# Seven products of half blocks in place of eight for the later batches' softmax times w_in

## The chip, the cores and the metric

The kernel runs on one NeuronCore of a Trainium2 chip. The metric is device microseconds (us) of one execution. The kernel before takes 716.05 us, the median of four runs that lie between 715.83 and 716.17 us.

## The reference

Two layers follow each other. The first is attention across channels: per batch `b` (4 batches, N = 6080 rows, C = 256 channels), the columns of q and k are normalised over the rows, `s = kn.T @ qn / tau` is a 256 x 256 matrix, a softmax over its last axis gives `a`, and the result is `v @ a`. The second layer works on all 24,320 rows:

```python
qn = q / (norm(q, axis=1) + 1e-6);  kn = k / (norm(k, axis=1) + 1e-6)
a  = softmax(kn.transpose(0, 2, 1) @ qn / tau, axis=-1)      # 4 x 256 x 256
x  = (v @ a).reshape(24320, 256)
h  = x @ w_in                                                # 256 -> 2048
g  = s * relu(h)**2 + b
out = g @ w_out                                              # 2048 -> 256
```

## The kernel before, in words

**Folding.** `v @ a @ w_in` is computed as `v @ (a @ w_in)`. For each batch the kernel makes one folded weight `wa`, 256 x 2048 in fp16, held as 128 partitions x 2 row halves x 2048 columns, and then never forms `x`. A batch's `e` (the exponentials, fp16, held transposed in the tile `eT`) is multiplied with `w_in`, and the row sums' reciprocals `rs` scale the result when it is read out of PSUM (the accumulator memory [...] that VectorE and ScalarE read).

**The main loop.** The rows are cut into 48 groups of 512 (the last has 256). A group is 16 steps; step `s` is group `s // 16`, place `m = s % 16`. A step does, in this order on TensorE:

- `mm1` (line 667): two matmuls of 512 columns that give one 128-row slice of `h` from `wa` and the transposed `v`;
- seven of the 112 matmuls of 128 columns (line 838) with which the group before is multiplied by `w_out`. That product already uses a seven-product scheme (`seven_items`): seven products X, Z, X, Y, X, Z, X of 16 matmuls each, with four sums S1 to S4 of blocks of `g` and four combinations T1, T2, T3, N4 of blocks of `w_out`. It starts at m = 3 and ends at m = 2 of the next group;
- what the table `side` holds for this step: the attention work of the next batch.

ScalarE does one relu of 1024 columns out of PSUM at each odd m (line 677), and at m = 3 and m = 5 a square besides (line 688). VectorE does three squares of 2048 columns per group (m = 0, 8, 12; line 690), the four sums S1 to S4 (m = 2, 3, 6, 10; lines 765 to 771), and the seven read-outs of the `w_out` products (line 695: at m = 5, 7, 9, 12, 14 and at m = 0 and 2 of the next group, by the count of 16 matmuls per product and seven per step). `h` has two PSUM tiles, so `mm1` of an even m needs the relu of four steps before; relu writes to two buffers `r16`, each freed by a square.

**The order of work.** Each engine runs its instructions in the order in which the program writes them (`po`, `keep_in_program_order`), one queue per engine; there is no planner. `at_step(s, f)` puts a piece of work at the end of step `s`. For batches 1 to 3 the Gram matrix `k.T @ q`, the norms and then `finish_ops` are laid out this way. With `first_group[b]` = 11, 23, 35 and `w1 = 16 * first_group[b] - 3`, the finish begins at `w1 - 54`, and its i-th piece stands at `w1 - 54 + 1 + FIN[i]`, or 3 steps apart after the end of `FIN`.

**The finish of a later batch.** The pieces are: copy the Gram matrix out, sum the norms, four activations for the inverse norms, scale, two exponentials, `sums` (row sums and their reciprocal, at `FIN` 22, which is m = 14), and then eight folds (`fold_one`): four blocks of 512 columns of `w_in` times two row halves. Each fold is two matmuls of 128 x 128 by 128 x 512 (line 328), accumulated over the two halves of the contraction in one PSUM bank, and one read-out that multiplies by `rs` and writes fp16 into `wa`: by ScalarE for m = 0 (line 321), by VectorE for m = 1 (line 323). The bank comes from the pool `ps_gram`, which has a single buffer, so a fold can start only when the read-out before it is done. The folds stand at m = 1, 4, 7, 10, 13, 0, 3 and 6 (`FIN[-1] + 3 * ...`). The result is first needed by `mm1` of group `first_group[b]`.

**Buffers.** The last three chunks of batch 0's norms (`NLATE` = 3) square q and k into `late_pool`, three buffers of 4096 bytes per partition that nothing uses afterwards.

Of the kernel before, what the change touches and what calls it, by code (L numbers as in the profile page):

```python
# [17 lines left out]
def kernel(  # L18
# [37 lines left out]
    def po(ins):  # L56

        tc.keep_in_program_order(ins)
        return ins

    def pool(name, bufs, **kw):
        return ctx.enter_context(tc.tile_pool(name=name, bufs=bufs, **kw))
# [3 lines left out]
    wpool = pool("wpool", 1)  # L66
    qk_pool = pool("qk_pool", 8)
    sq_pool = pool("sq_pool", 2)
    late_pool = pool("late_pool", NLATE)
    f3_pool = pool("f3_pool", 13)  # L70
    sm_pool = pool("sm", 1)
    apool = pool("apool", 2)
# [3 lines left out]
    gpool = pool("gpool", 2)  # L76
    spool = pool("spool", 1)
    upool = pool("upool", 4)
    opool = pool("opool", 2)

    ps_gram = pool("ps_gram", 1, space=PSUM)
# [29 lines left out]
    class Gram:  # L111
# [45 lines left out]
        def norm_ops(self, c):  # L157

            qc, kc = self.tiles[c]
            _, np_, jc = self.chunks[c]  # L160
            st = {}

            at_end = self.b == 0 and c >= len(self.chunks) - NLATE

            def squares(a, js):
                def f():
                    if "sq" not in st:
                        st["sq"] = (late_pool if at_end else sq_pool).tile(
                            [P, 2, JC, C], FP16, tag="sq", name="sq")
                    if a == 1 and at_end and c == len(self.chunks) - 1:  # L170
                        po(nc.vector.tensor_mul(
                            st["sq"][:np_, 1, js, :], kc[:np_, js, :], kc[:np_, js, :]))
                    elif a == 0 and (self.b > 0 or at_end or c % 2 == 0):
                        po(nc.vector.tensor_mul(  # L174
                            st["sq"][:np_, 0, js, :], qc[:np_, js, :], qc[:np_, js, :]))
                    else:
                        po(nc.scalar.activation(  # L177
                            out=st["sq"][:np_, a, js, :], in_=(qc, kc)[a][:np_, js, :],
                            func=AF.Square))
                return f  # L180

            def fold(half, arrays, last):
                def f():
                    src = st["f", 2 * half] if 2 * half < jc else st["sq"]
                    if ("f", half) not in st:
                        if last:
                            t = f3_pool.tile([P, 2, 1, C], FP16, tag="f3", name="f3")
                        else:
                            t = sq_pool.tile([P, 2, half, C], FP16, tag=f"f{half}", name="f")
                        st["f", half] = t  # L190
                    po(nc.vector.tensor_add(  # L191
                        st["f", half][:np_, arrays], src[:np_, arrays, :half, :],
                        src[:np_, arrays, half : 2 * half, :]))
                    if last and c == 0:
                        self.first = st["f", half]
                    if last and (c == 0 or self.b > 0 and c == len(self.chunks) - 1):
                        for rows in self.rows:
                            rows.append((st["f", half], np_, 1))
                return f

            def into_first():

                dst, src = self.first[:np_], st["f", 1][:np_]
                if self.b == 0:
                    po(nc.vector.tensor_add(dst, dst, src))  # L205
                else:
                    po(nc.gpsimd.dma_start(out=dst, in_=src, accum_op=ALU.add))  # L207

            def unfolded(a):
                self.rows[a].append((st["sq"], np_, jc))  # L210

            ops = []
            for h in range(0, jc, 4):
                js = slice(h, min(h + 4, jc))
                ops += [squares(1, js), squares(0, js)]
            if at_end:
                def rows(a):
                    if a == 0 or jc == 2:
                        return unfolded(a)
                    half = sq_pool.tile([P, 2, 2, C], FP16, tag="f2", name="half")  # L220
                    po(nc.vector.tensor_add(half[:np_, 1], st["sq"][:np_, 1, :2], st["sq"][:np_, 1, 2:]))
                    self.rows[1].append((half, np_, 2))
                return ops + [rows]
            if jc == 8:
                ops += [fold(4, slice(0, 1), False), fold(4, slice(1, 2), False)]
            ops += [fold(2, slice(0, 2), False), fold(1, slice(0, 2), True)]
            return ops + [into_first] if 0 < c < len(self.chunks) - 1 else ops
# [24 lines left out]
        def finish_ops(self):  # L252
# [3 lines left out]
            def inverse(a=None):  # L256

                n = C + CH if a is None else (CH, C)[a]

                def part(i):  # L260
                    if i == 0:
                        st["r", a] = sm_pool.tile([P, n], FP32, tag=f"r{a}", name=f"r{a}")
                        if a is None:
                            st["r", 1], st["r", 0] = st["r", a][:, :C], st["r", a][:, C:]
                    r = st["r", a]
                    func, kw = [(AF.Ln, dict(bias=tiny)), (AF.Exp, dict(scale=0.5)),
                                (AF.Ln, dict(bias=eps)), (AF.Exp, dict(scale=-1.0))][i]
                    sums = self.n_all if a is None else self.n_ps[a]
                    po(nc.scalar.activation(out=r, in_=r if i else sums, func=func, **kw))  # L269
                    if i == 3 and a != 1 and inv_tau != 1.0:  # L270
                        po(nc.vector.tensor_scalar_mul(
                            out=st["r", 0], in0=st["r", 0], scalar1=inv_tau))

                return [lambda i=i: part(i) for i in range(4)]
# [78 lines left out]
            def fold_one(f0, n, m):  # L353
                def f():
                    wa_ps = self.bank("wa_ps", CH, C).rearrange("p a c -> p (a c)")[:, :n]
                    fold_mm(f0, n, m, wa_ps)
                    if self.b == 0 and f0 == 2 * NW and m == 1:
                        return at_step(5, lambda: scaled(f0, n, m, wa_ps))
                    scaled(f0, n, m, wa_ps)
                return f  # L360

            if self.b == 0:
                blocks = [(2 * P, 2 * P), (4 * P, 2 * P), (6 * P, 2 * P), (2 * NW, NW), (3 * NW, NW)]
            else:
                blocks = [(f0, NW) for f0 in range(0, Dff, NW)]
            folds = [fold_one(f0, n, m) for f0, n in blocks for m in range(CH)]
            if self.b == 0:
                return [norms(1), *inverse(1), norms(0), *inverse(0), lambda: scale(CH),
                        lambda: first_block(2 * P)] + folds
            return [copy_out, norms_both, *inverse(), scale, lambda: exps(0), lambda: exps(1),  # L370
                    sums] + folds

        def bank(self, name, a, b):

# [189 lines left out]
        po(nc.scalar.copy(out=T[:, ts(i, 2), :], in_=w[:, 0, :, :P] if T is T2 else w[:, 0, :, P:]))  # L564


    side, early = {}, {}

    def at_step(s, f):
        side.setdefault(int(s), []).append(f)  # L570


    FIN = (0, 3, 5, 7, 9, 11, 13, 17, 19, 22)
    first_group = [b * N // TG for b in range(B)]
    FOLDS = (0, 0, 1, 1, 3, 3, 5, 5, 8, 8)
    for i, f in enumerate(folds):
# [30 lines left out]
    for b in range(1, B):  # L607
        gr = grams[b]
        w0 = first_group[b - 1] * FT + (26 if b == 1 else 6)
        w1 = first_group[b] * FT - 3  # L610
        NCH = len(gr.chunks)
        fin_len = 54
        span = (w1 - fin_len) - w0 - 12
        n = NCH * JC
        for c in range(NCH):
            sc = w0 + span * c * JC / n
            at_step(max(3, sc - 16), lambda gr=gr, c=c: gr.load(c))
            if c == 0:
                at_step(sc, gr.start)
            for j in range(JC):  # L620
                at_step(w0 + span * (c * JC + j) / n, lambda gr=gr, c=c, j=j: gr.mm(c, j))

            def norm_step(gr=gr, c=c, sc=sc):
                ops = gr.norm_ops(c)
                later = LATER.get((gr.b, c), {})
                for i, f in enumerate(ops):
                    at_step(int(sc) + 3 + i * 3 + later.get(i, 0), f)
            at_step(sc - 3, norm_step)

        def fin_step(gr=gr, s=w1 - fin_len):  # L630
            ops = gr.finish_ops()
            for i, f in enumerate(ops):
                at_step(int(s) + 1 + (FIN[i] if i < len(FIN) else FIN[-1] + 3 * (i - len(FIN) + 1)), f)
        at_step(w1 - fin_len - 12, fin_step)


# [298 lines left out]
```

## Time and profile before

| | |
|---|---|
| median of the runs shown | 716.05 us (715.83 to 716.17) |
| profiled execution | 716.16 us, its span 714.4 us |
| TensorE (PE) busy | 694.4 us, 97% of the span |
| weight loads (PEld) busy | 503.1 us, 70% |
| VectorE (DVE) busy | 623.2 us, 87% |
| ScalarE (ACT) busy | 545.7 us, 76% |
| granted TensorE clock | 0.997 of full speed |

The span runs from the first to the last instruction of the profiled execution; 1.8 us of that execution's time lie around it. "Busy" counts the time in which an engine works on an instruction. Consecutive instructions on an engine overlap a little (a VectorE row of 1.22 us is followed after 1.14 us), so a row's duration is somewhat more than the room it takes in its queue. Below, "starts" are given in us from the start of the span.

### The profile page before, as it was taken

What the parts mean: (1) busy time and instruction counts of PE and PEld (TensorE: products, weight loads), DVE (VectorE), ACT (ScalarE), POOL (GpSimd) and SP (SyncE); (2) the same over time, 40 slices, a digit from 0 to 9 for tenths busy, and PEclk for the clock granted to TensorE, in tenths of its full rate; (3) what the DMA queues carried; (4) which work ended last, traced back from release to release, by engine and by line L of the source; (5) the groups of instructions that cost most, each with busy time, mean ns of one, the idle gap of its engine ahead of it and who ended that gap; (6) DMA issues with size and microseconds to landing.
All of it is one profiled execution on the core that took longest, in us unless ns stands there. A gap on an engine that the chain in (4) does not pass through costs nothing.

```text
span 714.4 us, 17525 instructions
## 1 busy us (share of the span) xinstructions
PE 694.4 (97%) x7437; PEld 503.1 (70%) x7437; DVE 623.2 (87%) x877; ACT 545.7 (76%) x593; POOL 111.0 (16%) x189
## 2 busy tenths in 40 slices
PE   4699999999999999999999999999999999999998
PEld 2456777776777777777677777777668777777777
DVE  4889999988888989998889899998887888888886
ACT  5789877787777777778777777777877777777875
POOL 4533132102102222101010222110000000000000
PEclk9999999999999999999999999999999999999999
DMA  9999998637575989445772888943323333321202
GB/s 234 207 259 172 172 175 133 132 77 126 103 132 109 132 139 148 105 89 102 138 142 50 148 134 147 132 90 82 94 63 75 94 71 75 97 61 46 82 31 75
DMA packets 87454, 83.47 MB, mean 117 GB/s; under 512 B 56304, under 2 KB 62384, under 8 KB 87376
## 3 DMA queue, kind: packets, MB, share of 16 engines
q0 software_dynamic: 26608, 43.40, 38.0%
q1 hardware_dynamic: 60192, 37.71, 21.8%
q8 instruction: 58, 0.95, 0.6%
q10 hardware_dynamic: 576, 1.25, 0.5%
q14 instruction: 20, 0.16, 0.1%
HBM read 78.91 MB, written 24.90 MB: 145 GB/s over the span
## 4 chain that ended last, share of the span: by engine, by line
PE 95%; DMA 3%; ACT 1%; DVE 1%; issue 0%; DVEq 0%; ACTq 0%
PE h_ps L667 46%; PE o_ps L838 40%; PE s_ps L148 4%; PE wa_ps L328 2%; DMA qk<-in_k_dram 1%; DMA raw<-in_q_dram 1%; PE o_ps L742 1%; ACT sq L177 1%; PE o_ps L714 0%; DVE f L191 0%; ACT r L269 0%; PE n_ps L244 0%; ACT qk L139 0%; DVE f L205 0%; DVE sq L174 0%
## 5 line engine op out<-in xcount | busy, mean ns | idle before, releaser
L677 ACT ACTIVATE r<-h_ps 128x1024 f16<-128x1024 f32 (+1 forms) x384 | 388.8, 1014 | 148.8 <-PE h_ps L667 142.8
L667 PE MATMUL h_ps<-vT,wa 128*128 128x512 f16 (+7 forms) x1632 | 452.1, 364 | 0.5 <-ACT wa L321 0.5
L838 PEld LDWEIGHTS <-S 128*128 128x128 f16 x2944 | 198.0, 98 | 84.3
L838 PEld LDWEIGHTS <-g 128*128 128x128 f16 x2208 | 155.1, 98 | 74.2
L690 DVE TENSOR_TENSOR g<-r 128x2048 f16<-128x2048 f16 (+2 forms) x150 | 174.5, 1163 | 12.3 <-ACT r L677 11.9
L838 PE MATMUL o_ps<-T,S 128*128 128x128 f16 x2208 | 183.0, 219 | 0.0
L667 PEld LDWEIGHTS <-wa 128*128 128x128 f16 x1632 | 135.8, 98 | 19.7 <-ACT wa L321 1.0
L838 PE MATMUL o_ps<-w_out,g 128*128 128x128 f16 x1472 | 134.2, 219 | 0.0
L695 DVE SCALAR_TENSOR_TENSOR o_sb<-o_ps,s_out,u 128x256 f32<-128x256 f32 x138 | 66.3, 480 | 51.5 <-PE o_ps L838 49.5
L688 ACT ACTIVATE g<-r 128x1024 f16<-128x1024 f16 (+1 forms) x97 | 100.3, 1034 | 0.2
L148 PE MATMUL s_ps<-qk 128*128 128x256 f16 (+1 forms) x384 | 70.9, 286 | 14.9 <-ACT qk L139 9.3
L389 POOL DMA_DIRECT2D v<-in_v_dram x48 | 30.5, 637 | 264.4 <-DMA vT<-v 195.6
L695 DVE SCALAR_TENSOR_TENSOR u<-o_ps,s_out,rowconst 128x256 f32<-128x256 f32 x138 | 65.7, 476 | 0.0
L838 PE MATMUL o_ps<-w_out,S 128*128 128x128 f16 x736 | 63.5, 219 | 0.0
L838 PE MATMUL o_ps<-N,g 128*128 128x128 f16 x736 | 63.4, 219 | 0.0
L207 POOL DMA_DIRECT2D f<-f x30 | 26.4, 878 | 224.8 <-DVE f L191 175.2
L767 DVE TENSOR_TENSOR S<-S,g 128x2048 f16<-128x2048 f16 (+1 forms) x47 | 56.4, 1200 | 1.3
L177 ACT ACTIVATE sq<-qk 128x1024 f16<-128x1024 f16 (+2 forms) x53 | 54.5, 1041 | 3.9 <-DMA qk<-in_k_dram 2.4
L765 DVE TENSOR_TENSOR S<-g 128x2048 f16<-128x2048 f16 (+1 forms) x47 | 56.0, 1192 | 0.0
L771 DVE TENSOR_TENSOR S<-g,S 128x2048 f16<-128x2048 f16 x46 | 55.8, 1214 | 0.0
L769 DVE TENSOR_TENSOR S<-g 128x2048 f16<-128x2048 f16 x46 | 55.8, 1214 | 0.0
L148 PEld LDWEIGHTS <-qk 128*128 128x128 f16 (+1 forms) x384 | 32.5, 102 | 20.9 <-ACT qk L139 9.8
(83 smaller groups left out, 313.6 us busy)
## 6 DMA issues: line engine op xcount, KB each, us to landing
out_dram<-o_sb SPq DMA_DIRECT2D x43, 512.0 KB, 3.0
v<-in_v_dram POOLq DMA_DIRECT2D x47, 256.0 KB, 4.6
qk<-in_k_dram POOLq DMA_DIRECT2D x42, 256.0 KB, 6.8
qk<-in_q_dram POOLq DMA_DIRECT2D x42, 256.0 KB, 7.4
f<-f POOLq DMA_DIRECT2D x30, 128.0 KB, 3.1
vT<-v SPq DMA_TRANSPOSE x182, 2.9
w<-in_moe_w_out_dram POOLq DMA_DIRECT2D x4, 512.0 KB, 9.8
out_dram<-o_sb SPq DMA_DIRECT2D x8, 256.0 KB, 5.5
```

Source lines behind the costliest of these rows:

```text
L148: po(nc.tensor.matmul(self.s_ps[:, ch, :], qc[:np_, j, ts(ch, P)], kc[:np_, j, :], start=(c == 0 and j == 0 and ch == 0), stop=(c == len(s ...
L177: po(nc.scalar.activation(out=st["sq"][:np_, a, js, :], in_=(qc, kc)[a][:np_, js, :], func=AF.Square))
L667: po(nc.tensor.matmul(dst, wa[:, ci, ts(m, P)], src, start=(ci == 0), stop=(ci == CH - 1), skip_group_check=True))
L677: po(nc.scalar.activation(out=r16[:, :, i % 2, :n], in_=h_tiles.pop((g, i))[:, :, :n], func=AF.Relu))
L688: po(nc.scalar.activation(out=dst, in_=src, func=AF.Square))
L690: po(nc.vector.tensor_mul(dst, src, src))
L695: po(nc.vector.scalar_tensor_tensor(out=dst, in0=src, scalar=s_out, op0=ALU.mult, in1=add, op1=ALU.add))
L765: po(nc.vector.tensor_add(T[1], A21, A22))
L767: po(nc.vector.tensor_sub(T[2], T[1], A11))
L769: po(nc.vector.tensor_sub(T[3], A11, A21))
L771: po(nc.vector.tensor_sub(T[4], A12, T[2]))
L838: po(nc.tensor.matmul(st[name][:, j, :], a()[:, i, ts(j, P)], w[:, i, :], start=first, stop=last, skip_group_check=True))
```

## The change

Only batches 1 to 3 change; batch 0 keeps its folds.

- A 256 x 256 matrix times a 256 x 1024 pair of column blocks is a product of 2 x 2 blocks: two row halves and two contraction halves of `e`, and the contraction halves and the lower and upper 1024 columns of `w_in`. It is now computed by seven block products in place of eight, in two parts `p` of 512 columns (`seven_folds(0)`, `seven_folds(1)`).
- Each product is one matmul of 512 columns and stands at its own step. A product that is not marked new accumulates onto what the bank holds, after that has been read out: products 1 to 4 add up in one bank, product 5 has a bank of its own (the pool still has one buffer), products 6 and 7 add up in one.
- Each product has one read-out. Products 1, 2 and 3 are kept as fp32 tiles `u1`, `u2`, `u3` (1 and 3 by ScalarE, 2 by VectorE); product 4 goes to `wa` by ScalarE; products 5, 6 and 7 go to `wa` by VectorE, which multiplies by `rs` and adds `u1`, `u3` or `u2` in one instruction.
- `half_sums` makes four sums of 128 x 128 blocks of `e` on VectorE, right after the reciprocal, per batch. `w_in_sums` makes four combinations of 128 x 1024 blocks of `w_in` on VectorE, once, during batch 1's finish, at steps 6, 8 (two of them) and 22 after the finish begins. They are stored in the buffers of `late_pool`, which now have one tag per late chunk and that chunk's own size.
- `FIN` gets 14 entries (25 to 55) for the 14 products: m = 1, 3, 7, 9, 11, 13, 15, the same in two consecutive groups. The last stands one step before group `first_group[b]` begins.

```diff
@@ -66,7 +66,7 @@
     wpool = pool("wpool", 1)
     qk_pool = pool("qk_pool", 8)
     sq_pool = pool("sq_pool", 2)
-    late_pool = pool("late_pool", NLATE)
+    late_pool = pool("late_pool", 1)
     f3_pool = pool("f3_pool", 13)
     sm_pool = pool("sm", 1)
     apool = pool("apool", 2)
@@ -76,6 +76,7 @@
     gpool = pool("gpool", 2)
     spool = pool("spool", 1)
     upool = pool("upool", 4)
+    fold_pool = pool("fold_pool", 1)
     opool = pool("opool", 2)
 
     ps_gram = pool("ps_gram", 1, space=PSUM)
@@ -165,8 +166,10 @@
             def squares(a, js):
                 def f():
                     if "sq" not in st:
-                        st["sq"] = (late_pool if at_end else sq_pool).tile(
-                            [P, 2, JC, C], FP16, tag="sq", name="sq")
+                        if at_end:
+                            st["sq"] = late_pool.tile([P, 2, jc, C], FP16, tag=f"sq{c}", name="sq")
+                        else:
+                            st["sq"] = sq_pool.tile([P, 2, JC, C], FP16, tag="sq", name="sq")
                     if a == 1 and at_end and c == len(self.chunks) - 1:
                         po(nc.vector.tensor_mul(
                             st["sq"][:np_, 1, js, :], kc[:np_, js, :], kc[:np_, js, :]))
@@ -359,16 +362,77 @@
                     scaled(f0, n, m, wa_ps)
                 return f
 
+            def half_sums():
+
+                A = lambda m, k: st["e"][:, k, ts(m, P)]
+                S = st["S"] = [fold_pool.tile([P, P], FP16, tag=f"S{n}", name=f"S{n}")
+                               for n in range(1, 5)]
+                po(nc.vector.tensor_add(S[0], A(1, 0), A(1, 1)))
+                po(nc.vector.tensor_sub(S[1], S[0], A(0, 0)))
+                po(nc.vector.tensor_sub(S[2], A(0, 0), A(1, 0)))
+                po(nc.vector.tensor_sub(S[3], A(0, 1), S[1]))
+
+            def seven_folds(p):
+
+                A = lambda m, k: st["e"][:, k, ts(m, P)]
+                B = lambda k, n: w_in16[:, k, ds(n * (Dff // 2) + p * NW, NW)]
+                T = lambda n: W[n][:, ts(p, NW)]
+                S = lambda n: st["S"][n - 1]
+                C_ = lambda m, n: self.wa[:, m, ds(n * (Dff // 2) + p * NW, NW)]
+                rs = lambda m: st["rs"][:, m : m + 1]
+                u = {}
+
+                def product(a, w, then, new=False):
+                    def f():
+                        if new:
+                            st["wa_ps"] = self.bank("wa_ps", CH, C).rearrange("p a c -> p (a c)")
+                        po(nc.tensor.matmul(st["wa_ps"], a(), w(), start=new, stop=True,
+                                            skip_group_check=True))
+                        then()
+                    return f
+
+                def keep(n, m):
+                    def f():
+                        u[n] = fold_pool.tile([P, NW], FP32, tag=f"u{n}", name=f"u{n}")
+                        if n == 2:
+                            po(nc.vector.tensor_scalar_mul(
+                                out=u[n], in0=st["wa_ps"], scalar1=rs(m)))
+                        else:
+                            po(nc.scalar.mul(out=u[n], in_=st["wa_ps"], mul=rs(m)))
+                    return f
+
+                def out(m, n, k=None):
+                    def f():
+                        if k is None:
+                            po(nc.scalar.mul(out=C_(m, n), in_=st["wa_ps"], mul=rs(m)))
+                        else:
+                            po(nc.vector.scalar_tensor_tensor(
+                                out=C_(m, n), in0=st["wa_ps"], scalar=rs(m), op0=ALU.mult,
+                                in1=u[k], op1=ALU.add))
+                    return f
+
+                return [
+                    product(lambda: A(0, 0), lambda: B(0, 0), keep(1, 0), True),
+                    product(lambda: S(2), lambda: T("T2"), keep(2, 0)),
+                    product(lambda: S(3), lambda: T("T3"), keep(3, 1)),
+                    product(lambda: A(1, 1), lambda: T("N4"), out(1, 0)),
+                    product(lambda: A(0, 1), lambda: B(1, 0), out(0, 0, 1), True),
+                    product(lambda: S(1), lambda: T("T1"), out(1, 1, 3), True),
+                    product(lambda: S(4), lambda: B(1, 1), out(0, 1, 2)),
+                ]
+
             if self.b == 0:
                 blocks = [(2 * P, 2 * P), (4 * P, 2 * P), (6 * P, 2 * P), (2 * NW, NW), (3 * NW, NW)]
-            else:
-                blocks = [(f0, NW) for f0 in range(0, Dff, NW)]
-            folds = [fold_one(f0, n, m) for f0, n in blocks for m in range(CH)]
-            if self.b == 0:
+                folds = [fold_one(f0, n, m) for f0, n in blocks for m in range(CH)]
                 return [norms(1), *inverse(1), norms(0), *inverse(0), lambda: scale(CH),
                         lambda: first_block(2 * P)] + folds
+
+            def sums_and_halves():
+                sums()
+                half_sums()
+
             return [copy_out, norms_both, *inverse(), scale, lambda: exps(0), lambda: exps(1),
-                    sums] + folds
+                    sums_and_halves] + seven_folds(0) + seven_folds(1)
 
         def bank(self, name, a, b):
 
@@ -564,13 +628,31 @@
         po(nc.scalar.copy(out=T[:, ts(i, 2), :], in_=w[:, 0, :, :P] if T is T2 else w[:, 0, :, P:]))
 
 
+    W = {}
+
+    def w_in_sums(i):
+
+        F = Dff // 2
+        B = lambda k, n: w_in16[:, k, ds(n * F, F)]
+        if not W:
+            c0, c1, c2 = range(NCH0 - NLATE, NCH0)
+            W["T1"] = late_pool.tile([P, F], FP16, tag=f"sq{c1}", name="T1w")
+            W["T2"] = late_pool.tile([P, F], FP16, tag=f"sq{c2}", name="T2w")
+            both = late_pool.tile([P, 2, F], FP16, tag=f"sq{c0}", name="TNw")
+            W["T3"], W["N4"] = both[:, 0], both[:, 1]
+        po([lambda: nc.vector.tensor_sub(W["T1"], B(0, 1), B(0, 0)),
+            lambda: nc.vector.tensor_sub(W["T2"], B(1, 1), W["T1"]),
+            lambda: nc.vector.tensor_sub(W["T3"], B(1, 1), B(0, 1)),
+            lambda: nc.vector.tensor_sub(W["N4"], B(1, 0), W["T2"])][i]())
+
     side, early = {}, {}
 
     def at_step(s, f):
         side.setdefault(int(s), []).append(f)
 
 
-    FIN = (0, 3, 5, 7, 9, 11, 13, 17, 19, 22)
+    FIN = (0, 3, 5, 7, 9, 11, 13, 17, 19, 22,
+           25, 27, 31, 33, 35, 37, 39, 41, 43, 47, 49, 51, 53, 55)
     first_group = [b * N // TG for b in range(B)]
     FOLDS = (0, 0, 1, 1, 3, 3, 5, 5, 8, 8)
     for i, f in enumerate(folds):
@@ -630,7 +712,10 @@
         def fin_step(gr=gr, s=w1 - fin_len):
             ops = gr.finish_ops()
             for i, f in enumerate(ops):
-                at_step(int(s) + 1 + (FIN[i] if i < len(FIN) else FIN[-1] + 3 * (i - len(FIN) + 1)), f)
+                at_step(int(s) + 1 + FIN[i], f)
+            if gr.b == 1:
+                for i, later in ((2, 6), (0, 8), (1, 8), (3, 22)):
+                    at_step(int(s) + later, lambda i=i: w_in_sums(i))
         at_step(w1 - fin_len - 12, fin_step)
```

## The prediction

> **What bounds the kernel now.** I read the page first, then TensorE's waits, the groups by shape, the busy time of the fold stage, and the timelines around the first fold of batch 1.
>
> ```profile
> span 714.4 us, 17525 instructions
> ...
> PE 694.4 (97%) x7437; PEld 503.1 (70%) x7437; DVE 623.2 (87%) x877; ACT 545.7 (76%) x593; POOL 111.0 (16%) x189
> ...
> PE   4699999999999999999999999999999999999998
> ...
> PE 95%; DMA 3%; ACT 1%; DVE 1%; issue 0%; DVEq 0%; ACTq 0%
> ```
>
> TensorE is full from the third slice on, and the chain that ended last is 95% TensorE. The 20 us in which it is not busy lie in front: its waits, longest first in total, are five rows; these four and one of 0.3 us.
>
> ```profile
> PE s_ps L148 <- ACT qk L139: 9.3, 2, 7.5
> PE s_ps L148 <- DMA qk<-in_q_dram: 5.6, 6, 1.5
> PE n_ps L244 <- DVE half L221: 1.3, 1, 1.3
> PE h_ps L667 <- ACT wa L321: 0.5, 1, 0.5
> ```
>
> All belong to batch 0. The busy times in the stretch that holds batch 1's folds (us; PE, PEld, DVE, ACT, POOL) say the same, and show the room beside TensorE: about 5 us on VectorE, 8 on ScalarE.
>
> ```profile
> 163.40:193.90 30.50, 30.50 (x317) 20.83 (x315) 25.55 (x35) 22.17 (x25) 3.00 (x7) 1.00 0.65 121
> ```
>
> So a matmul removed here shortens the run by its own pace, as long as no read-out makes TensorE wait. Groups by shape (busy us, mean ns) give the durations:
>
> ```profile
> L690 DVE TENSOR_TENSOR g<-r 128x2048 f16<-128x2048 f16 x137 | 166.6, 1216 | 10.0 <-ACT r L677 9.7
> L695 DVE SCALAR_TENSOR_TENSOR o_sb<-o_ps,s_out,u 128x256 f32<-128x256 f32 x138 | 66.3, 480 | 51.5 <-PE o_ps L838 49.5
> L328 PE MATMUL wa_ps<-w_in,eT 128*128 128x512 f16 x56 | 16.3, 379 | 0.0
> L323 DVE TENSOR_SCALAR wa<-wa_ps,rs 128x512 f16<-128x512 f32 x14 | 10.4, 744 | 0.0
> L321 ACT ACTIVATE wa<-wa_ps,rs 128x512 f16<-128x512 f32 x14 | 9.6, 684 | 0.0
> L690 DVE TENSOR_TENSOR g<-r 128x1024 f16<-128x1024 f16 x9 | 6.2, 687 | 1.9 <-ACT r L677 1.8
> L695 DVE SCALAR_TENSOR_TENSOR o_sb<-o_ps,s_out,rowconst 128x512 f32<-128x512 f32 x2 | 1.4, 746 | 0.1
> ```
>
> The timeline of TensorE (start, length) shows a fold between two steps; the 379 ns of a matmul are latency, its pace is read from starts.
>
> ```profile
> 165.12 0.59 PE L667 MATMUL h_ps<-vT,wa 128*128 128x512 f16 x2
> 165.55 0.55 PE L838 MATMUL o_ps<-N,g 128*128 128x128 f16 x7
> 165.94 0.59 PE L328 MATMUL wa_ps<-w_in,eT 128*128 128x512 f16 x2
> 166.38 0.59 PE L667 MATMUL h_ps<-vT,wa 128*128 128x512 f16 x2
> ```
>
> From 165.94 to 166.38 (0.432 before rounding) are two matmuls: 0.216 each. A step without a fold is 0.432 for `mm1` plus 0.39 for seven small ones, 0.822.
>
> **What the skill says.** "TensorE: Matmul & The Clock Gate", section "Back-to-back issue gap", gives a 512-column matmul 512/2.4 + 2.5 = 216 ns; this trace agrees. "PSUM — Partial Sum Buffer", section "The four PSUM rules", allows a synchronised read of a partial sum inside an accumulation group, so products 2, 3, 4 and 7 may add onto a bank that has been read; each must wait for that read, and no run here shows it yet. "VectorE: DVE Perf Modes", section "Side-by-side: where the cycles go for N=2048 bf16", makes a 16-bit tensor_tensor two elements per cycle plus some 150 cycles: 1224 ns for 2048, the trace has 1216; for the 128-column half sums, which the trace lacks, I take (64 + 150)/0.96 = 223 ns as an estimate, between 0.15 (the reciprocal of 2 columns, 157 ns) and 0.42 (the 512-column row of line 690, 418 ns).
>
> **The change on TensorE.** Per batch 8 folds x 2 = 16 matmuls go, 2 parts x 7 = 14 come: two fewer. Three batches: 6 x 0.216 = **1.30 us less**. Each product keeps one weight load of 98 ns; loads lie beside matmuls (PEld 68% in that stretch) and six of them go too.
>
> **The read-outs.** Per batch ScalarE goes from four to six of 0.684 (0.57 of room, as the next row starts 0.1 before the end), VectorE from four to eight: two plain of 0.744, six with an added operand. Does the operand cost? At 256 columns rows of line 695 with `u` take 480 ns, with `rowconst` 476 to 482; so I price 512 columns at the 746 of the last row above (0.66 of room). VectorE's load per group in the fold stage, in room: three squares and four sums at 1.14 plus 0.12 for the dependent pair S1, S2, 8.1; seven read-outs at 0.395, 2.8; four fold read-outs at 0.66, 2.6: 13.5 us. A group lasts 16 x 0.822 + 7 x 0.216 = 14.66. It fits, with 1.1 to spare. ScalarE: eight relus at 0.92, two squares at 0.94, three read-outs at 0.57: 10.9.
>
> **Whether a product waits.** All products use the one bank, so each must find the read-out before it finished. Products are 0.216 + 2 x 0.822 = 1.86 us apart, except 3.50 between the second and third. I place them on the clock of batch 1, first product at 165.94 as before, each engine's queue in program order:
>
> - Product 1 (m = 1): ScalarE reads it after this step's relu, 166.67 to 167.35 as the fold there today. Product 2 starts at 167.80: 0.45 to spare.
> - Product 2 (m = 3): VectorE reads it behind S1 and S2, which follow the read-out of the last `w_out` product (167.18); 169.97 to 170.71. Product 3 at 171.31: 0.60.
> - Product 3 (m = 7): ScalarE is behind here, two squares at m = 3 and 5: relu at 171.33, read-out 172.25 to 172.94. Product 4 at 173.18: **0.24**, the least. Today's fold at m = 7 has it likewise:
>
> ```profile
> 171.78 1.01 ACT L677 ACTIVATE r<-h_ps 128x1024 f16<-128x1024 f32 x1
> 172.68 0.69 ACT L321 ACTIVATE wa<-wa_ps,rs 128x512 f16<-128x512 f32 x1
> ```
>
> - Product 4 (m = 9): read by 174.59, product 5 at 175.05: 0.46.
> - Product 5 (m = 11): behind S4, read 175.45 to 176.19, product 6 at 176.92: 0.73.
> - Product 6 (m = 13): behind the m = 12 read-out and square, read 177.64 to 178.38, product 7 at 178.79: 0.41.
> - Product 7 (m = 15): read by 179.91; the next part's product 1 at 180.65: 0.74.
>
> VectorE then waits again for the next group's last `w_out` product, so nothing is carried into part two or the next batch. Behind a late read-out would stand the m = 14 read-out and the squares, whose buffer the relu at m = 13 or m = 1 needs; they end more than 2 us before it. The last write into `wa` (about 1 us into the next group) concerns columns used at m = 12 to 15, 10 us later. The Gram bank is next needed seven steps on. No DMA or queue of SP or POOL moves. The stage makes no waits: 0.
>
> **The sums.** Half sums: 4 x 0.22 = 0.9 us per batch right after the reciprocal, where VectorE sits idle 1.24 us before 165.21. Hidden; without that cover they would put off S1 by 0.9. `w_in_sums`, once: four of 0.687 (0.60 of room). The last, at m = 13, falls before the same gap; the 0.3 that spill over end in the gap of 0.57 before 167.40. The other three (m = 13 and twice m = 15 of the group before, the second of the pair dependent, +0.12) come to 1.92 us from 150.22. The gaps there hold 1.25 (before 151.95) and 0.23 (before 153.71). S1 would begin at 154.46, not at
>
> ```profile
> 154.11 1.22 DVE L765 TENSOR_TENSOR S<-g 128x2048 f16<-128x2048 f16 x1
> 155.69 0.44 PE L838 MATMUL o_ps<-T,S 128*128 128x128 f16 x5
> ```
>
> so it ends at 155.68, while TensorE's first use of it stands at 155.69 with its weight load 0.05 ahead. I take a wait of **0.10 us**, once; bounds 0 and 0.4 (if the small gap gives nothing).
>
> **Sum.** Against its own execution (716.16; 714.4 of span and 1.8 around): -1.30 + 0.10 = -1.20, so 713.2 of span and 714.96; the median of the runs lies 0.11 lower, 716.05, so **714.85**, 0.17% less. `late_pool`'s three tags keep three buffers for three chunks: 0.
>
> **Rivals.**
> - *Handover waits eat part of the gain.* The 0.24 at product 4 and 0.41 at product 7 assume that a release costs nothing. For: a square waiting on a relu starts 0.03 after it, but TensorE waiting on ScalarE is seen only in batch 0. With 0.4 per release, product 4 waits 0.16 six times, about 0.9 in all: 715.8.
> - *VectorE becomes the bound, slower.* Place: the six three-operand read-outs per batch. If the fp32 `u` stream costs a pass of its own, three per group exceed the spare 1.1 us. Price: at 1.5 us each, 3 x 0.75 - 1.1 = 1.15 per group, six groups 6.9: 716.05 - 1.2 + 6.9, about 721.5. From 1.28 us each (1.6 over per group, 0.5 late, 3 us in all) the result is slower than before. Against: 480 against 476 ns at 256 columns.
> - *TensorE is not what sets the pace there*, and the saved matmuls turn into idle: 716.05. Against: 30.50 busy of 30.50.
>
> **How the numbers follow.** Forecast 0.65, own range 714.55 to 715.2; handover waits 0.20; no gain 0.03; VectorE bound 0.12. A measurement here tells about 0.2%, 1.43 us, from no change, and the whole matmul gain is 1.30: only the low tail of the forecast counts as faster, 0.14; slower is the VectorE case, 0.12; the rest, 0.74, is within 0.2%. The range, 714.4 to 716.5, holds all but the last case and a little of each edge.
>
> **What would show it.** Line 328's matmuls for batches 1 to 3 fall from 48 to 42 with 0.216 between starts; TensorE's waits gain no row above 0.2 us; three-operand read-outs near 0.75 us; VectorE's gap near 151 filled, a wait of about 0.1 us at 155.7. A TensorE wait on the kept tiles, on `wa` or at product 4, or read-outs above 1.1 us, would prove it wrong.

## The result, and the profile after

The changed kernel takes 715.09 us (median of 42 runs, 714.83 to 715.58) against 715.97 for the kernel before in the same sessions: 0.88 us less, ratio 0.9988 with a 95% interval of 0.9984 to 0.9993. That is within 0.2%, in the lower half of the forecast range (714.4 to 716.5) and inside the narrower one (714.55 to 715.2); the forecast was 714.85, a gain of 1.20.

The page of the changed kernel's profiled execution (715.08 us) begins:

```profile
span 713.3 us, 17540 instructions
...
PE 692.3 (97%) x7431; PEld 502.2 (70%) x7431; DVE 634.7 (89%) x905; ACT 548.5 (77%) x599; POOL 110.9 (16%) x189
```

TensorE has six matmuls less (7431 for 7437), VectorE 28 instructions and 11.5 us more, ScalarE six and 2.8 us more. The busy times of batch 1's fold stage, same columns as for the kernel before, show where the room went: VectorE from 25.55 to 28.50 us of 30.50.

```profile
163.40:193.90 30.50, 30.50 (x321) 21.05 (x319) 28.50 (x43) 23.80 (x28) 3.88 (x8) 1.00 0.62 124
```

Groups by shape of the changed kernel (busy us, mean ns): the read-outs that add an operand, the two kinds that are kept, the last of `w_in`'s sums, one of the half sums.

```profile
L409 DVE SCALAR_TENSOR_TENSOR wa<-wa_ps,rs,u 128x512 f16<-128x512 f32 x18 | 13.5, 749 | 3.4 <-PE wa_ps L389 3.4
L401 ACT ACTIVATE u<-wa_ps,rs 128x512 f32<-128x512 f32 x12 | 8.2, 686 | 0.0
L398 DVE TENSOR_SCALAR u<-wa_ps,rs 128x512 f32<-128x512 f32 x6 | 4.5, 744 | 0.0
L646 DVE TENSOR_TENSOR TNw<-w_in,T2w 128x1024 f16<-128x1024 f16 x1 | 0.7, 679 | 0.0
L373 DVE TENSOR_TENSOR S<-eT,S 128x128 f16<-128x128 f16 x3 | 0.7, 218 | 0.0
```

Now the waits. TensorE's wait list has the same five rows as before; nothing of the change is in it, and by this list the prediction's sign, no new row above 0.2 us, is met. But the timeline of the two engines in batch 1's finish (start, length) has a hole:

```profile
157.66 1.22 DVE L854 TENSOR_TENSOR S<-g 128x2048 f16<-128x2048 f16 x1
158.80 0.47 DVE L780 SCALAR_TENSOR_TENSOR u<-o_ps,s_out,rowconst 128x256 f32<-128x256 f32 x1
```

```profile
158.74 0.50 PE L923 MATMUL o_ps<-T,S 128*128 128x128 f16 x6
159.33 0.22 PE L923 MATMUL o_ps<-w_out,g 128*128 128x128 f16 x1
159.38 0.59 PE L752 MATMUL h_ps<-vT,wa 128*128 128x512 f16 x2
```

Six matmuls of 0.056 us from 158.74 are issued by 159.07, and the next starts only at 159.33: 0.253 us lost. The last of the six is still shown as busy until 159.24, since a matmul of pace 0.056 is shown with a length of 0.219, so the wait list sees hardly any idle time (0.09). Waits this short must be read from starts. I define a wait as the distance of two starts less the pace of the first matmul, and leave out the first 60 us and two gaps near 78 and 100 us that every kernel here has (0.18 to 0.20 together). The kernel before has no others. The changed kernel has:

| start, us | TensorE waits before | us |
|---|---|---|
| 155.5 | first use of S1, batch 1, product Z | 0.037 |
| 159.0 | first matmul of product Y, batch 1 | 0.253 |
| 171.2, 185.9, and the same in batches 2 and 3 | second pass of product X, once per fold group | 0.130 in six |

(The second pass of X is the third `w_out` product, which adds onto what the first left in PSUM, once that has been read out.)

That is 0.420 in all, and 6 x 0.216 - 0.420 = 0.876 us of gain, against 0.88 measured. What remains to be shown is what those waits are, and that there is nothing else.

### The profile page after: what moved, and what is told of

It reads as the page before. It is cut to its first block, busy times and chain, and to the rows that moved or that the text cites. A ratio compares the mean times of both kernels' runs of the same rounds, so it can differ in the third digit from the quotient of the medians.

```text
span 713.3 us, 17540 instructions
## 1 busy us (share of the span) xinstructions
PE 692.3 (97%) x7431; PEld 502.2 (70%) x7431; DVE 634.7 (89%) x905; ACT 548.5 (77%) x599; POOL 110.9 (16%) x189
## 3 DMA queue, kind: packets, MB, share of 16 engines
q10 hardware_dynamic: 576, 1.25, 0.5%
## 4 chain that ended last, share of the span: by engine, by line
PE 92%; DVE 3%; DMA 3%; ACT 2%; issue 0%; DVEq 0%; ACTq 0%
PE h_ps L752 45%; PE o_ps L923 39%; PE s_ps L149 4%; DMA qk<-in_k_dram 1%; PE wa_ps L389 1%; DMA raw<-in_q_dram 1%; PE o_ps L827 1%; ACT sq L180 1%; PE o_ps L799 0%; PE wa_ps L331 0%; DVE f L194 0%; DVE g L775 0%; ACT r L272 0%; ACT g L773 0%; ACT r L762 0%
```

## The experiments

### The read-out of Z comes late

```diff
-    FIN = (0, 3, 5, 7, 9, 11, 13, 17, 19, 22,
+    FIN = (0, 3, 5, 7, 9, 11, 15, 17, 19, 22,
```

> The scaling of the Gram matrix moves from m = 5 to m = 7, behind the read-out of product Z, all else as in the changed kernel. My theory: the 0.25 us that TensorE loses near 159.2 in batch 1 is product Y's first matmul waiting for VectorE's read-out of Z, which lies in the same PSUM bank and which the w_in sums made late. With the 0.60 us of scaling behind it, the read-out comes in time: that wait falls to 0, the 0.04 before the first use of S1 stays, the six waits of 0.02 in the fold groups stay; the time falls by about 0.25, to 714.85. Rival: the wait hangs on the sums S1 to S3 or on relu; then 0.25 stays and the time is 715.1.

Measured: 714.74 us against 715.86 for the kernel before, 1.12 less, ratio 0.9984 (0.9977 to 0.9991). The wait at 159 is gone, the one at S1 is 0.045, the six small ones stay (0.142 in all). So the releaser of product Y is VectorE's read-out of Z: Y and Z are two halves of one PSUM tile. (The move brings S3 forward too, but Y multiplies `g` with `w_out`, and in the changed kernel S3 was done at 158.88, 0.45 before Y started.) In the changed kernel the read-out of Z ends at 159.273 and Y's matmul starts at 159.327, 0.054 later: call this the handover. The kernel before had the read-out at 158.63 to 159.11 and Y at 159.21, only 0.05 us to spare beyond such a handover:

```profile
158.63 0.48 DVE L695 SCALAR_TENSOR_TENSOR u<-o_ps,s_out,rowconst 128x256 f32<-128x256 f32 x1
```

```profile
158.87 0.50 PE L838 MATMUL o_ps<-T,S 128*128 128x128 f16 x6
159.21 0.22 PE L838 MATMUL o_ps<-w_out,g 128*128 128x128 f16 x1
```

### The sums of w_in

```diff
-                for i, later in ((2, 6), (0, 8), (1, 8), (3, 22)):
+                for i, later in ((2, 6), (0, 8), (1, 22), (3, 24)):
```

> Two of the four combinations of w_in move 14 and 2 steps: T3 and T1 stay at steps 6 and 8 of batch 1's finish, T2 goes to step 22 and N4 to step 24; all else as in the changed kernel. My theory: T3 and T1 need 1.2 us of room and VectorE's gap there is 1.25, so both waits of batch 1 (0.25 at product Y, 0.04 at S1) vanish; T2 and N4 with the half sums put S1 of the next group off by 0.2 to 0.4 us, which its slack there covers. Time about 714.8. Rival: the waits come from something else than the w_in sums (the shorter start of the run, a relu), and 0.25 to 0.29 stays: 715.1.

Measured: 714.77 us, 1.09 less than before, ratio 0.9985 (0.9978 to 0.9991). Both waits of batch 1's early finish are gone, so `w_in`'s three sums in one gap caused them. One of the six small waits grew from 0.021 to 0.101 (at 170.8): with the sums that moved, VectorE has no idle time left before that read-out of X, and what is late there is no longer S1 but the second pass of X.

### The six small waits

```diff
-           25, 27, 31, 33, 35, 37, 39, 41, 43, 47, 49, 51, 53, 55)
+           25, 27, 29, 31, 33, 35, 37, 39, 41, 43, 45, 47, 49, 51, 53, 55)
...
-                    product(lambda: S(2), lambda: T("T2"), keep(2, 0)),
+                    product(lambda: S(2), lambda: T("T2"), lambda: None),
+                    keep(2, 0),
```

> VectorE's read-out of product 2 is written two steps later (m = 5 in place of m = 3), behind the read-out of the first w_out product; products stay where they are. My theory: the six waits of 0.02 us (one per fold group, at the first matmul of the third w_out product, X) come from the read-out of X standing behind the 0.66 us of product 2's read-out; they vanish, 0.13 us in all, and product 3 still finds its bank free with about 0.2 to spare. The two waits of batch 1 stay. Time about 714.95. Rival: the 0.02 are a cost of TensorE's own at the changed weights; then they stay, or product 3 now waits, and the time is 715.1 or more.

Measured: 714.85 us, 1.01 less than before, ratio 0.9985 (0.9978 to 0.9991). All six are gone, and product 3 does not wait. The two waits of batch 1 stay (0.041 and 0.256). In the changed kernel the read-out of X, put off by product 2's 0.66 us, ends at 171.227, and X's next matmul starts at 171.281: again 0.054. It is the fifth matmul of the last TensorE row here; VectorE and TensorE, first the kernel before, then the changed one:

```profile
170.85 0.47 DVE L695 SCALAR_TENSOR_TENSOR u<-o_ps,s_out,rowconst 128x256 f32<-128x256 f32 x1
171.35 0.55 PE L838 MATMUL o_ps<-T,S 128*128 128x128 f16 x7
```

```profile
170.09 0.74 DVE L398 TENSOR_SCALAR u<-wa_ps,rs 128x512 f32<-128x512 f32 x1
170.75 0.47 DVE L780 SCALAR_TENSOR_TENSOR u<-o_ps,s_out,rowconst 128x256 f32<-128x256 f32 x1
171.04 0.57 PE L923 MATMUL o_ps<-T,S 128*128 128x128 f16 x7
```

A fold's read-out stood ahead of X's in this group before, too (170.19), and from the start of VectorE's last `w_out` read-out to the end of X's it is 3.93 us in both kernels. But TensorE now has one matmul in that stretch where a fold had two, and comes 0.216 sooner: the 0.248 us between X's read-out and X's matmul shrink to 0.032, less than a handover. In this group the gain itself makes the wait. In the second group of each batch a fold's read-out did not stand there before (X's followed S2 directly, from 185.51), and product 2's is new work.

### All three moves

> The three moves together (scaling at m = 7, w_in sums apart, product 2's read-out at m = 5). My theory: TensorE has no wait left after batch 0's start, so the full price of six matmuls, 1.30 us, is seen against the kernel before: 714.65 to 714.7, ratio 0.9982. Rival: part of the difference of 1.30 and the 0.88 that was measured is not in waits but in the products' own cost; then about 0.3 of it stays and the time is 715.0.

Measured: 714.57 us against 715.86, 1.29 less, ratio 0.9982 (0.9976 to 0.9989). That is clear of the kernel before. Against the changed kernel the intervals overlap (0.9976 to 0.9989 and 0.9984 to 0.9993), and what tells the two apart is the trace: no wait is left beyond the two near 78 and 100 us. The timeline around product Y and the first fold group's X shows the room that the three moves make:

```profile
158.04 0.48 DVE L781 SCALAR_TENSOR_TENSOR u<-o_ps,s_out,rowconst 128x256 f32<-128x256 f32 x1
158.44 0.68 DVE L297 TENSOR_TENSOR sm_t<-sm_t,rNone 128x512 f32<-128x512 f32 x1
...
170.07 0.48 DVE L781 SCALAR_TENSOR_TENSOR u<-o_ps,s_out,rowconst 128x256 f32<-128x256 f32 x1
170.47 0.74 DVE L398 TENSOR_SCALAR u<-wa_ps,rs 128x512 f32<-128x512 f32 x1
```

```profile
158.89 0.50 PE L924 MATMUL o_ps<-T,S 128*128 128x128 f16 x6
159.22 0.22 PE L924 MATMUL o_ps<-w_out,g 128*128 128x128 f16 x1
```

The read-out of Z is done at 158.52, 0.70 before product Y; six matmuls take from 158.89 to 159.22 and the seventh follows at once.

### Is TensorE the pace? Six matmuls given back

```diff
-                        po(nc.tensor.matmul(st["wa_ps"], a(), w(), start=new, stop=True,
-                                            skip_group_check=True))
+                        for _ in range(2 if again else 1):
+                            po(nc.tensor.matmul(st["wa_ps"], a(), w(), start=new, stop=True,
+                                                skip_group_check=True))
```

(The other lines of this edit make `again` an argument of `product` and set it for the first product of each part alone.)

> The first product of each part is computed twice, the same matmul of 512 columns issued two times in a row, so TensorE has six matmuls more than in the changed kernel and as many as in the kernel before. My theory: TensorE sets the pace in this stage, so each costs 0.216 us: 1.30 us more than the changed kernel, less up to 0.13 because the six waits of 0.02 us find cover; 716.25 to 716.4, slower than the kernel before by the 0.3 to 0.4 us of waits. Rival: TensorE is not what sets the pace there and the matmul fills idle time; then 715.1.

Measured: 716.32 us against 715.93, ratio 1.0006 (0.9998 to 1.0015). The median is 0.39 us over the kernel before; the interval alone does not separate the two. The trace does: with as many matmuls as before, the waits sum to 0.432. Against the changed kernel the intervals do not touch: 0.88 below its kernel before there, 0.39 above it here, so six matmuls cost 1.27 us, 1.30 by their pace. The six small ones found no cover, unlike what I allowed for. Six matmuls are worth their pace, and the third rival, that they turn into idle time, is out.

### A product that comes too early

```diff
-           25, 27, 31, 33, 35, 37, 39, 41, 43, 47, 49, 51, 53, 55)
+           25, 27, 31, 32, 35, 37, 39, 41, 43, 47, 48, 51, 53, 55)
```

> Product 4 stands at m = 8 in place of m = 9 in both parts, before ScalarE's read-out of product 3 can be done. It measures what a product pays that comes too early, and what the release from ScalarE to TensorE costs. By the trace of the changed kernel product 3's read-out ends at 173.05 and product 4 would start at 172.49: a wait of 0.56 us plus the handover, six times. My theory: the handover is under 0.1, so 0.56 to 0.66 each, part of it given back because later waits shrink: 3 to 4 us in all, 718 to 719. Rival (handover waits, 0.2 to 0.4 per release): 0.8 to 0.96 each, 5 us or more, 720 and over.

Measured: 718.75 us (one run). Product 4 waits 0.613 to 0.621 in each of the six groups. ScalarE and TensorE in the first:

```profile
172.35 0.69 ACT L401 ACTIVATE u<-wa_ps,rs 128x512 f32<-128x512 f32 x1
```

```profile
172.09 0.55 PE L923 MATMUL o_ps<-T,S 128*128 128x128 f16 x7
173.09 0.38 PE L389 MATMUL wa_ps<-TNw,eT 128*128 128x512 f16 x1 [0.45 <-ACT u L401]
```

The read-out ends at 173.042, the product starts at 173.093: a handover of 0.051, and 0.050 or 0.051 in the other five groups. So a product that adds onto a bank in mid-sum does wait until the bank has been read, and the price of 0.2 to 0.4 per release is out. The list says 0.45 where 0.615 were lost, for the reason given above.

### How much room VectorE has

```diff
+                            if (m, n) in ((0, 1),):
+                                spare = fold_pool.tile([P, NW], FP16, tag="spare", name="spare")
+                                po(nc.vector.scalar_tensor_tensor(
+                                    out=spare, in0=st["wa_ps"], scalar=rs(m), op0=ALU.mult,
+                                    in1=u[k], op1=ALU.add))
```

> VectorE's read-out of product 7 is done twice in each part (once into a spare tile), 0.66 us more of room per fold group; the result is not changed. By the trace VectorE is idle 0.93 us per fold group. My theory: 0.66 fits, TensorE gains no wait over 0.1 us per group, time 715.1 to 715.6. Rival (VectorE is already the bound): 0.66 x 6 = 4 us more, 719.

Measured: 716.07 us (one run), more than expected. Part of it is this run's start, long before the folds: its gap near 78 us lies 0.36 later than in the changed kernel's profile. The waits sum to 1.024 in place of 0.420, 0.10 more per fold group: X's second pass waits 0.17 in the second group of each batch, and the group after it 0.03. So 0.66 us does not fit for nothing, though 0.93 are idle: the idle time is three pieces (0.36, 0.17, 0.40), and only the one between product 7's read-out and the next read-out of X, 0.36, can take this work.

With the read-outs of products 5, 6 and 7 all done twice, each first into a spare tile:

> All three read-outs with an added operand (products 5, 6 and 7) are done twice in each part, 3 x 0.66 = 1.98 us more of room on VectorE per fold group against 0.93 us of idle time. This is the size of my slower rival, in which such a read-out takes two passes. My theory: VectorE is then the bound by about 1.05 us per group, six groups, so 4 to 6.5 us over the changed kernel, 719 to 721.6, slower than the kernel before. Rival: buffers and slack between groups take it up, and the time stays under 716.

Measured: 721.57 us (one run), 5.6 over the kernel before, at the edge of what I expected. But not in the way expected. TensorE's waits now have a row of this change, and the timeline shows the place:

```profile
PE wa_ps L389 <- DVE wa L414: 4.9, 6, 0.8
```

```profile
178.33 0.74 DVE L411 SCALAR_TENSOR_TENSOR spare<-wa_ps,rs,u 128x512 f16<-128x512 f32 x1
178.99 0.74 DVE L414 SCALAR_TENSOR_TENSOR wa<-wa_ps,rs,u 128x512 f16<-128x512 f32 x1
179.65 0.47 DVE L785 SCALAR_TENSOR_TENSOR o_sb<-o_ps,s_out,u 128x256 f32<-128x256 f32 x1
180.21 0.75 DVE L411 SCALAR_TENSOR_TENSOR spare<-wa_ps,rs,u 128x512 f16<-128x512 f32 x1
```

```profile
179.79 0.38 PE L389 MATMUL wa_ps<-w_in,S 128*128 128x512 f16 x1 [0.82 <-DVE wa L414]
```

Product 7 waits 0.985 us for product 6's read-out in each group, 5.9 of 7.1 us of waits. VectorE is even idle for a moment before 180.21. So most of the loss is at one product's bank, not in VectorE's total load.

### The balance

Matmuls at 0.216 each, plus the waits read from each kernel's trace, against the measured difference to the kernel before of the same session:

| kernel | matmuls | waits | sum | measured |
|---|---|---|---|---|
| the change | -1.296 | 0.420 | -0.88 | -0.88 |
| scaling later | -1.296 | 0.187 | -1.11 | -1.12 |
| sums apart | -1.296 | 0.218 | -1.08 | -1.09 |
| read-out of product 2 later | -1.296 | 0.297 | -1.00 | -1.01 |
| all three | -1.296 | 0 | -1.30 | -1.29 |
| first product twice | 0 | 0.432 | 0.43 | 0.39 |
| product 4 early (one run) | -1.296 | 4.136 | 2.84 | 2.82 |
| last read-out twice (one run) | -1.296 | 1.024 | -0.27 | 0.14 |
| three read-outs twice (one run) | -1.296 | 7.06 | 5.76 | 5.64 |

But for the one run with the late start, matmuls and waits account for everything within 0.12 us. The measured differences of the medians have 95% intervals of 0.3 to 0.6 us on either side, and the waits come from one trace each, so an agreement to 0.01 or 0.02 is partly luck. What carries the argument is that each wait was there or gone in the trace as the move said.

## Why the prediction was right, and where its sum was off

- **The matmuls** were right: 1.30 us predicted, 1.29 measured once nothing waits. The Trainium skill ("TensorE: Matmul & The Clock Gate", section "Back-to-back issue gap"), which the prediction quotes, gives this 216 ns for an isolated matmul, and about 131 ns at 512 columns for a stream of weight loads and matmuls. Here every matmul has its weight load (7431 of each) and starts are still 0.216 us apart, so only the first of the two figures fits.
- **The read-outs** were right: 746 ns were taken for the added operand, 749 measured. Half sums were put at 223 ns, and are 200 to 226. The slower rival fell with this. (Its price, 716.05 - 1.2 + 6.9, is 721.75 and not 721.5.)
- **The seven products' waits** were right: none waits, and the time from each read-out to the next product is within 0.07 us of what was worked out. At product 4, the tightest, it is 0.25 where 0.24 was worked out (read-out until 173.05, product at 173.31), and 0.20 beyond a handover.
- **That a release costs nothing** was wrong, though by 0.05 us and not by the 0.4 of the handover rival. No product pays it. The second pass of X does: without a handover it would have had 0.03 to spare. So this rival came true in small, at a place that it did not name.
- **The wait at S1** was predicted at 0.10 and is 0.037. S1 began where it was put: at 154.28 on a clock 0.18 ahead, which is 154.46. (The gaps of 1.25 and 0.23 as quoted would give 154.55; the first holds 1.34 of room, as a read-out takes 0.39 of its queue and not 0.48.) TensorE was ahead by the same 0.18, so that is not why the wait is short. The weight load of S1, which stood 0.054 ahead of its matmul, came 0.087 late, and the matmul followed it after 0.004: only 0.037 of the delay reached the matmuls.
- **The failed step** is "The sums": the prediction follows the late VectorE to the end of S1 and stops. VectorE had next to no idle time after it, so the same 0.35 us reached S2, the read-out of X, the scaling, S3 and then the read-out of Z, which product Y's first matmul needs because Y shares Z's tile. There 0.35 of delay met 0.05 to spare, on a TensorE that was itself 0.04 later: 0.26 by this sum, 0.253 measured, where the prediction had nothing.
- **The stage "makes no waits: 0"** was off by 0.130: the prediction compared each product with the read-out before it, but not the `w_out` product X with its read-out, which stands behind product 2's.
- **Room on VectorE** was put at 1.1 us per group and is 0.93. Taking it as one sum was the greater error, as the doubled read-outs show: by them the slower rival would have set in earlier, at one product's bank; at which duration was not measured.

So the mechanism was right, a saving of the matmuls' pace less waits that VectorE makes; the term for waits, 0.10, measured 0.42, of which 0.037 lies at the place that was named. That the time still fell into the narrower range is due to the smallness of this term, not to its being right.

## What to carry to other kernels

On a saturated engine, a change is worth the pace of what it removes less every wait that it makes, and both can be read from starts to hundredths of a microsecond; a wait list that counts idle time misses much of a wait when the work before it is shown with more than its pace (0.219 for 0.056 here). When work is put into a queue, follow each later instruction of that queue until the queue next idles, and compare each with the moment at which somebody needs it, buffer mates included. Room in a queue is not a sum: only the idle piece between the insertion and the next deadline counts. And what is taken off the busy engine brings its next demand forward: a margin elsewhere can shrink by what was saved, as X's did.

## What the runs showed of the hardware

A matmul that waited for a PSUM bank started almost the same time after the end of the instruction that freed it, however long the wait: 0.050 to 0.051 us after ScalarE in six waits (product 4 early), 0.052 to 0.055 after VectorE in every wait of 0.02 to 0.99 us that batches 1 to 3 have in these runs. Where the weight load waits instead (S1), the load starts 0.054 after the end of the sum and the matmul 0.058 after it.

The added 512-column fp32 operand from SBUF costs a VectorE read-out of PSUM nothing that shows: product 6's read-outs take 743 to 744 ns, plain ones, of product 2, 743 to 746. The 750 to 751 ns of products 5 and 7, which make the mean of 749, are all read-outs that start after idle time. Writing fp32 in place of fp16 costs ScalarE nothing either: 681 to 682 ns for product 1 (fp32) and 681 to 683 for product 4 (fp16); product 3's 689 to 692 (fp32) were 689 to 692 at the same place in the kernel before, in fp16.
